# Multiplying half of the value chunks in 32 bits, unsplit, with a column of ones

## The chip, the cores and the metric

The kernel runs on one core of one Trainium2 chip. TensorE (PE) multiplies and writes its results to PSUM, VectorE (DVE) and ScalarE (ACT) compute on SBUF and PSUM, GpSimd (POOL) on SBUF alone, and SyncE (SP) issues nearly all DMAs. The metric is the device time of one execution in microseconds.

## What is computed

The reference is an attention through 49 agents in two steps, followed by a mixture of experts. There are 4 batches of 10048 tokens with 128 channels.

```python
a2k = sm(agents, k)          # softmax over the 10048 keys, with the scale 1/sqrt(128)
agent_v = a2k @ v            # 49 x 128 for each batch
q2a = sm(q, agents)          # softmax over the 49 agents
x = (q2a @ agent_v).reshape(B * N, D)
...
# each token goes to one group of four and one expert of four in it
h = np.maximum(xg[mask_e] @ w1[g, e], 0.0)
ye = h @ w2[g, e]
out[tok_idx] = combined[:, None] * ye
```

The change concerns `a2k @ v`: the sum over all keys of the weight of a key for each agent, times the value of that key, and the sum of the weights by which it is divided.

## The kernel before

The 10048 tokens of a batch are 79 tiles of 128 (the last one has 64), in 8 chunks of 10 tiles (the last of 9). The batches are taken in the order 1, 2, 3, 0. Precision comes from splitting: a 32-bit operand is written as a 16-bit part and a 16-bit remainder, and a product is the sum of three 16-bit products (high x high, high x low, low x high).

*The opening.* For the first batch everything is computed alone: `front` runs keys and values in an order written out by hand (`ORDER`). There the values are not split: `key_exp` loads a chunk of values to `vf`, of 129 columns, and sets the last column to one; `key_values` multiplies each tile in 32 bits, weights `S` (128 keys x 49 agents) stationary and `vf` moving, so that the product has 49 rows of 128 channels and the sum of the weights.

*The stream.* Then the expert layer of batches 1, 2 and 3 runs as a stream of units (`first`, `evicted`, `second`): two products of 512 columns into a bank `ph`, an eviction in two parts (`hh` by ScalarE, `hl` by VectorE), and three products of 512 columns into `po`. A batch has 20 tiles of 8 units. There are three `ph` banks, so TensorE runs at most three units ahead of the evictions. After each unit `advance` steps generators ("lanes") that prepare later batches: the keys and values of the next batch (`k1`, `k2`, `k3`), the queries (`q0` to `q3`), and what follows them. `QUEUE` says from which to which part of the stream a lane runs, `TOTALS` how much weighted work it has in all, `RATE` how much VectorE and ScalarE work one unit may take; `behind` compares the done share with the share of the window. After that a planner draws up every engine's queue anew, from the order of emission and its own estimate of when each operand is there; operations of one engine can change places in it.

*A k lane* is `agents`: `key_load` and `key_scores` for all chunks, `key_max`, and then for all chunks four stages run skewed by one chunk each: `value_load` (DMA to `vf`, two buffers) and `value_less` (subtract the maximum), `value_exp`, `value_split` and `value_products`. `value_split` writes `vh` and `sh` (ScalarE), `vl` in two pieces a chunk (VectorE), `sl` in two pieces (GpSimd), and adds the weights of chunks 1 to 7 onto those of chunk 0 in two pieces a chunk (GpSimd). `value_products` makes three products a tile, values stationary (128 x 128) and weights moving (49 columns), into the bank `acc`, 128 channels x 49 agents. At the end `agents` sums the weights over the 10 tiles of chunk 0 and over partitions by a product with ones, and divides. Only these three lanes are touched by the change; the opening isn't.

*The last batch* is sorted by expert and computed with gathered rows and scattered results, after the three streamed ones.

A helper records nearly all operations, so most rows carry its line, L137, and are told apart by their tiles.

Of the kernel before, what the change touches and what calls it, by code (L numbers as in the profile page):

```python
# [10 lines left out]
F32 = mybir.dt.float32  # L11
# [3 lines left out]
ALU = mybir.AluOpType  # L15
# [52 lines left out]
ORDER = "kkkkkmkvkvqkqmvvqvvvv"  # L68
RATE = np.array([900.0, 1100.0])
POOLED = "01001001"  # L70
KA = 2
QUEUE = (("a0", 0.0, 9.0), ("a1", 0.0, 9.0), ("a2", 0.0, 9.0), ("a3", 0.0, 9.0),
         ("q0", 0.0, 0.50), ("k1", 0.0, 0.60), ("q1", 0.40, 1.35), ("k2", 0.60, 1.15), ("q2", 1.30, 2.35), ("k3", 1.15, 1.70), ("q3", 1.55, 2.25), ("p3", 1.80, 2.72))
TOTALS = {"q0": 22.9e3, "k1": 55.1e3, "q1": 26.2e3, "k2": 55.1e3, "q2": 26.2e3, "k3": 55.1e3, "q3": 26.2e3, "p3": 79.0}
WL = (0.5, 1.0, 0.7)
AHEAD = 4
AHEAD_TURNS = 2
# [64 lines left out]
def build(ctx, tc, qT, kT, v, agT, wr, w1, w2, cpk, out, cols):  # L142
# [28 lines left out]
    def bank(any_=True):  # L171

        if wide[0] and any_:
            turns[0] += 1
            k = turns[0] % 8
            if k in (0, 3, 6):
                return ps1.tile([P, TS], F32, name="ph")
            if k in (1, 4):
                return ps2.tile([P, TQ, C], F32, name="po").rearrange("p a c -> p (a c)")
        return psa.tile([P, 512], F32, name="at", tag="at")  # L180
# [20 lines left out]
    vec.memset(ones16, 1.0)  # L201
    ones = const.tile([P, P], F32, name="ones")
    vec.memset(ones, 1.0)
    shift = const.tile([P, 1], F32, name="shift")
    vec.memset(shift, float(np.log(ES)))
    keep = const.tile([P, NE, ST], F16, name="keep")
# [222 lines left out]
    def value_load(b, ci):  # L429

        t0, t1 = chunks[ci]
        vf = stg.tile([P, CT, C + 1], F32, name="vf", tag="vf", bufs=2)
        nf = min(t1, NT - 1) - t0
        sync.dma_start(out=vf[:, 0:nf, 0:C], in_=v[b, t0 * P:(t0 + nf) * P].rearrange("(t p) c -> p t c", p=P))
        if t1 == NT:
            sync.dma_start(out=vf[0:LAST, nf, 0:C], in_=v[b, (NT - 1) * P:N])
        state[b]["v", ci] = vf
        yield

# [18 lines left out]
    def value_split(b, ci):  # L458

        st = state[b]  # L460
        vf = st.pop(("v", ci))
        sh, sl = [mo.tile([P, CT, NA], F16, name=name) for name in ("sh", "sl")]
        vh, vl = [wk.tile([P, CT * P], F16, name=name, tag="x" + name[1]).rearrange("p (t c) -> p t c", c=C) for name in ("vh", "vl")]
# [25 lines left out]
    def value_products(b, ci):  # L489

        st = state[b]
        sh, sl, vh, vl = st.pop(("v", ci))
        if ci == 0:
            st["acc"] = bank(False)
        acc = st["acc"]
        t0, t1 = chunks[ci]
        for t in range(t0, t1):
            m = min(P, N - t * P)
            i = t - t0
            for x, y in (vh, sh), (vh, sl), (vl, sh):  # L500
                pe.matmul(acc[:, 0:NA], x[0:m, i], y[0:m, i], start=(t == 0 and x is vh and y is sh), stop=False)
            if i % 5 == 4 or t == NT - 1:
                yield
        yield

    def agents(b):
# [5 lines left out]
        yield from skewed(n, lambda ci: both(value_load(b, ci), value_less(b, ci)), lambda ci: value_exp(b, ci), lambda ci: value_split(b, ci), lambda ci: value_products(b, ci))  # L512
        yield
        acc = st["acc"]
        sums = sm.tile([P, NA], F32, name="mx")
        vec.tensor_reduce(out=sums, in_=st["S"][:, 0:CT].rearrange("p t a -> p a t"), axis=AX.X, op=ALU.add)
        yield HOP
        pe.matmul(acc[:, NA:2 * NA], ones, sums, start=False, stop=True)
        yield HOP
        za = sm.tile([P, NA], F32, name="za2")  # L520
        vec.tensor_scalar(out=za, in0=acc[:, NA:2 * NA], scalar1=1e-9 * ES, scalar2=None, op0=ALU.add)
        vec.reciprocal(out=za, in_=za)
        avT = sm.tile([P, NA], F32, name="avT")
        vec.scalar_tensor_tensor(out=avT, in0=acc[:, 0:NA], scalar=1.0 / VS, in1=za, op0=ALU.mult, op1=ALU.mult)
        yield
        yield from agents_scaled(b, avT)

# [1080 lines left out]
```

## Time and profile before

| what | value |
|---|---|
| median of 3 runs (lowest to highest) | 939.1 us (936.59 to 939.77) |
| the profiled execution | 946.72 us |
| its span from first to last instruction | 945.0 us |
| TensorE busy, weight loads busy | 860.7 us (91%), 511.9 us |
| VectorE busy | 750.0 us (79%) |
| ScalarE busy | 623.1 us (66%) |
| GpSimd busy | 468.5 us (50%) |
| mean granted TensorE clock | 0.975 |

Durations of instructions come from the profiled execution, and so does every sum of them. A matmul's record contains its drain, so the records of short matmuls overlap, and the busy time of TensorE hides short waits; the distance from start to start tells what one costs in a run. The granted clock is a share of full speed: 1.0 is 2.4 GHz, 0.5 is 1.2 GHz.

### The profile page before, as it was taken

The numbers are of one execution on the slowest core, as the hardware profiler recorded it, in microseconds if no ns is written. First come the engines' busy times: TensorE is split into PE (matmuls) and PEld (weight loads), VectorE is DVE, ScalarE is ACT, GpSimd is POOL, SyncE is SP. The second block draws the span as 40 slices with busy tenths as digits, with TensorE's granted clock in tenths as the row PEclk, the third lists the DMA queues.
The fourth block names the chain that finished last, engine by engine and source line by source line (L and its number), as shares of the span: only waits on it lengthen the run. The fifth ranks groups of instructions, "written<-read, shape, count | busy, mean of one in ns | idle before, by whom it ended". The sixth has DMA issues, their size and how long they took to land.

```text
span 945.0 us, 22657 instructions
## 1 busy us (share of the span) xinstructions
PE 860.7 (91%) x8616; PEld 511.9 (54%) x8617; DVE 750.0 (79%) x1621; ACT 623.1 (66%) x1084; POOL 468.5 (50%) x618
## 2 busy tenths in 40 slices
PE   3878998999999889989799989999999999999994
PEld 2763554544555445544445555544444467777774
DVE  5647799898689898859988998989997666666662
ACT  4546787776878777768679867766566554555551
POOL 3164656653747343476547423656555414444444
PEclk9977999999999999989999999999999999999998
DMA  9637743746435554553534233333576435455542
GB/s 316 182 127 241 240 128 91 227 146 201 141 110 188 166 170 134 182 159 115 168 122 158 92 125 96 99 124 108 173 255 221 148 133 175 152 184 186 173 153 66
DMA packets 96495, 150.63 MB, mean 159 GB/s; under 512 B 8984, under 2 KB 61843, under 8 KB 96377
## 3 DMA queue, kind: packets, MB, share of 16 engines
q1 hardware_dynamic: 91225, 138.80, 46.0%
q0 software_dynamic: 5152, 10.30, 3.3%
q8 instruction: 69, 1.13, 0.5%
q14 instruction: 49, 0.40, 0.1%
HBM read 108.04 MB, written 39.69 MB: 156 GB/s over the span
## 4 chain that ended last, share of the span: by engine, by line
PE 54%; DVE 23%; issue 7%; POOL 7%; ACT 5%; DMA 3%; SPq 0%; POOLq 0%; ACTq 0%; DVEq 0%
PE po L137 28%; PE ph L137 16%; PE at L137 10%; DVE hl L137 8%; POOL xl L273 3%; DVE vl L137 3%; ACT hh L137 2%; POOL out L1286 2%; DVE oh L137 2%; DVE S L137 1%; DVE oo L137 1%; DVE mq L137 1%; ACT vh L137 1%; DVE ef L137 1%; POOL xs L273 1%
## 5 line engine op out<-in xcount | busy, mean ns | idle before, releaser
L137 DVE SCALAR_TENSOR_TENSOR hl<-ph,hh 128x512 f16<-128x512 f32 (+1 forms) x562 | 376.0, 676 | 127.6 <-ACT hh L137 111.3
L137 ACT ACTIVATE hh<-ph 128x512 f16<-128x512 f32 (+1 forms) x562 | 328.4, 592 | 194.2 <-PE ph L137 102.1
L137 PEld LDWEIGHTS <-wbuf 128*128 128x128 f16 (+2 forms) x2852 | 246.6, 98 | 297.8 <-issue 59.6
L137 PE MATMUL ph<-et,wbuf 98*128 98x512 f16 (+2 forms) x1048 | 319.1, 379 | 23.1 <-DVE hl L137 21.3
L137 PE MATMUL po<-hh,wbuf 128*128 128x512 f16 (+1 forms) x960 | 288.0, 379 | 2.7 <-DVE oo L137 2.1
L273 POOL TENSOR_TENSOR xl<-xf,xh 128x256 f16<-128x256 f32 x280 | 188.0, 706 | 154.5 <-ACT xh L137 144.3
L137 PE MATMUL po<-hl,wbuf 128*128 128x512 f16 (+1 forms) x480 | 181.7, 378 | 0.0
L1286 POOL DMA_INDIRECT out<-oo,er x82 | 80.4, 981 | 113.3 <-ACT hh L137 55.1
L137 PE MATMUL po<-wbuf,hh 128*128 128x128 f16 x1312 | 117.1, 219 | 0.5 <-issue 0.5
L137 PE MATMUL po<-wbuf,hl 128*128 128x128 f16 x656 | 113.0, 219 | 0.3 <-issue 0.2
L1013 POOL DMA_INDIRECT sorted_rows<-rows,slot x79 | 80.0, 1012 | 62.6 <-ACT hh L137 36.5
L137 PEld LDWEIGHTS <-hh 128*128 128x128 f16 x1312 | 99.2, 98 | 9.4 <-issue 9.3
L137 ACT ACTIVATE xh<-xf 128x1280 f16<-128x1280 f32 (+2 forms) x59 | 73.7, 1251 | 20.6 <-PE at L137 8.0
L137 PEld LDWEIGHTS <-xh 128*128 128x128 f16 (+1 forms) x1164 | 58.8, 99 | 23.3 <-issue 5.3
L719 POOL TENSOR_TENSOR rows<-ef,rows 128x245 f16<-128x245 f32 (+1 forms) x62 | 39.9, 666 | 60.7 <-ACT rows L137 60.7
L137 PEld LDWEIGHTS <-hl 128*128 128x128 f16 x656 | 64.2, 98 | 0.9 <-issue 0.9
L480 POOL TENSOR_TENSOR sl<-S,sh 128x245 f16<-128x245 f32 (+2 forms) x51 | 36.2, 733 | 51.5 <-ACT sh L137 40.1
L137 PE MATMUL at<-agh,xl 128*128 128x49 f16 x523 | 52.7, 186 | 5.6 <-POOL xl L273 5.4
L137 DVE SCALAR_TENSOR_TENSOR hl<-at,hh 128x512 f16<-128x512 f32 x82 | 55.8, 681 | 0.0
L137 PE MATMUL at<-agh,xh 128*128 128x49 f16 x523 | 52.7, 186 | 2.0 <-DVE base L137 1.4
L137 PEld LDWEIGHTS <-xl 128*128 128x128 f16 x582 | 48.9, 98 | 7.6 <-POOL xl L273 7.2
L137 ACT ACTIVATE et<-at 98x512 f16<-98x512 f16 (+2 forms) x80 | 47.2, 593 | 7.8 <-PE at L137 7.7
(277 smaller groups left out, 1188.5 us busy)
## 6 DMA issues: line engine op xcount, KB each, us to landing
wbuf<-wdr SPq DMA_DIRECT2D x22, 832.0 KB
vf<-v SPq DMA_DIRECT2D x28, 640.0 KB
xf<-qT SPq DMA_DIRECT2D x28, 640.0 KB
cols<-oo SPq DMA_DIRECT2D x60, 256.0 KB
xf<-kT SPq DMA_DIRECT2D x23, 640.0 KB
oo<-cwt SPq DMA_DIRECT2D x57, 256.0 KB
erow<-rows SPq DMA_DIRECT2D x12, 490.0 KB
er<-sorted_rows SPq DMA_DIRECT2D x19, 256.0 KB
```

The costliest lines, as they stand in the source:

```text
L137: return f(*a, **k)
L273: pool.tensor_sub(out=xl[:, a:z], in0=xf[:, a:z], in1=xh[:, a:z])
L480: pool.tensor_sub(out=sl[0:m, y][:, z], in0=x[:, z], in1=sh[0:m, y][:, z])
L719: pool.tensor_sub(out=x0[:, a:z, NA:2 * NA], in0=ef[:, a:z], in1=x0[:, a:z, 0:NA])
L1013: ins = pool.indirect_dma_start(out=sorted_rows[:, :], out_offset=bass.IndirectOffsetOnAxis(ap=at, axis=0), in_=x, in_offset=None, bounds_ ...
L1286: ins = pool.indirect_dma_start(out=out, out_offset=bass.IndirectOffsetOnAxis(ap=to, axis=0), in_=y, in_offset=None, bounds_check=N - 1, o ...
```

## The change

Of the eight chunks of values of each later batch, those with a "1" in `WHOLE` (1, 3, 4 and 6, ten tiles each) are no longer split. `value_load` sets the 129th column of their `vf` to one, `value_split` does nothing for them, and `value_products` multiplies `S` (stationary, 49 columns) with `vf` (moving, 129 columns) in 32 bits, one product a tile, into other columns and the first 49 rows of the same PSUM bank. The other four chunks go as before. GpSimd no longer adds the weights of the four chunks onto chunk 0; the column of ones gives their sum. At the end of a batch the 49 x 129 result is copied to SBUF, transposed and scaled by a product with `identv`, its sums are spread over the partitions by a product of ones with a diagonal matrix, and both are added to what the split chunks gave. `TOTALS` of the three k lanes is 46.8e3 instead of 55.1e3. A manual dependency without a semaphore keeps the first 32-bit product behind the one that opens the bank.

```diff
--- before.py
+++ after.py
@@ -68,10 +68,11 @@
 ORDER = "kkkkkmkvkvqkqmvvqvvvv"
 RATE = np.array([900.0, 1100.0])
 POOLED = "01001001"
+WHOLE = "01011010"
 KA = 2
 QUEUE = (("a0", 0.0, 9.0), ("a1", 0.0, 9.0), ("a2", 0.0, 9.0), ("a3", 0.0, 9.0),
          ("q0", 0.0, 0.50), ("k1", 0.0, 0.60), ("q1", 0.40, 1.35), ("k2", 0.60, 1.15), ("q2", 1.30, 2.35), ("k3", 1.15, 1.70), ("q3", 1.55, 2.25), ("p3", 1.80, 2.72))
-TOTALS = {"q0": 22.9e3, "k1": 55.1e3, "q1": 26.2e3, "k2": 55.1e3, "q2": 26.2e3, "k3": 55.1e3, "q3": 26.2e3, "p3": 79.0}
+TOTALS = {"q0": 22.9e3, "k1": 46.8e3, "q1": 26.2e3, "k2": 46.8e3, "q2": 26.2e3, "k3": 46.8e3, "q3": 26.2e3, "p3": 79.0}
 WL = (0.5, 1.0, 0.7)
 AHEAD = 4
 AHEAD_TURNS = 2
@@ -201,6 +202,8 @@
     vec.memset(ones16, 1.0)
     ones = const.tile([P, P], F32, name="ones")
     vec.memset(ones, 1.0)
+    identv = const.tile([NA, NA], F32, name="identv")
+    vec.tensor_scalar(out=identv, in0=identf[0:NA, 0:NA], scalar1=VS, scalar2=None, op0=ALU.mult)
     shift = const.tile([P, 1], F32, name="shift")
     vec.memset(shift, float(np.log(ES)))
     keep = const.tile([P, NE, ST], F16, name="keep")
@@ -434,6 +437,8 @@
         sync.dma_start(out=vf[:, 0:nf, 0:C], in_=v[b, t0 * P:(t0 + nf) * P].rearrange("(t p) c -> p t c", p=P))
         if t1 == NT:
             sync.dma_start(out=vf[0:LAST, nf, 0:C], in_=v[b, (NT - 1) * P:N])
+        if WHOLE[ci] == "1":
+            vec.memset(vf[:, :, C:C + 1], 1.0)
         state[b]["v", ci] = vf
         yield
 
@@ -458,6 +463,9 @@
     def value_split(b, ci):
 
         st = state[b]
+        if WHOLE[ci] == "1":
+            yield
+            return
         vf = st.pop(("v", ci))
         sh, sl = [mo.tile([P, CT, NA], F16, name=name) for name in ("sh", "sl")]
         vh, vl = [wk.tile([P, CT * P], F16, name=name, tag="x" + name[1]).rearrange("p (t c) -> p t c", c=C) for name in ("vh", "vl")]
@@ -489,16 +497,28 @@
     def value_products(b, ci):
 
         st = state[b]
+        t0, t1 = chunks[ci]
+        if WHOLE[ci] == "1":
+            vf = st.pop(("v", ci))
+            for t in range(t0, t1):
+                m = min(P, N - t * P)
+                ins = pe.matmul(st["acc"][0:NA, P:P + C + 1], st["S"][0:m, t], vf[0:m, t - t0], start=False, stop=False)
+                if t == t0:
+                    tc.add_manual_dep(ins.ins, st["opened"].ins.name, mybir.DependencyInfo(mybir.DependencyClass.NoSync, mybir.DependencyReason.DATA),
+                                      reason="the bank is opened by the first product")
+                if (t - t0) % 3 == 2 or t == t1 - 1:
+                    yield
+            return
         sh, sl, vh, vl = st.pop(("v", ci))
         if ci == 0:
             st["acc"] = bank(False)
         acc = st["acc"]
-        t0, t1 = chunks[ci]
         for t in range(t0, t1):
             m = min(P, N - t * P)
             i = t - t0
             for x, y in (vh, sh), (vh, sl), (vl, sh):
-                pe.matmul(acc[:, 0:NA], x[0:m, i], y[0:m, i], start=(t == 0 and x is vh and y is sh), stop=False)
+                ins = pe.matmul(acc[:, 0:NA], x[0:m, i], y[0:m, i], start=("opened" not in st), stop=(t == NT - 1 and x is vl))
+                st.setdefault("opened", ins)
             if i % 5 == 4 or t == NT - 1:
                 yield
         yield
@@ -512,16 +532,25 @@
         yield from skewed(n, lambda ci: both(value_load(b, ci), value_less(b, ci)), lambda ci: value_exp(b, ci), lambda ci: value_split(b, ci), lambda ci: value_products(b, ci))
         yield
         acc = st["acc"]
+        af = sm.tile([NA, C + 1], F32, name="af", bufs=1)
+        vec.tensor_copy(out=af, in_=acc[0:NA, P:P + C + 1])
+        dg = sm.tile([NA, NA], F32, name="dg")
+        vec.tensor_scalar(out=dg, in0=identf[0:NA, 0:NA], scalar1=af[:, C:C + 1], scalar2=None, op0=ALU.mult)
         sums = sm.tile([P, NA], F32, name="mx")
         vec.tensor_reduce(out=sums, in_=st["S"][:, 0:CT].rearrange("p t a -> p a t"), axis=AX.X, op=ALU.add)
         yield HOP
-        pe.matmul(acc[:, NA:2 * NA], ones, sums, start=False, stop=True)
+        ps = bank()
+        pe.matmul(ps[:, 0:NA], af[:, 0:C], identv, start=True, stop=False)
+        pe.matmul(ps[:, NA:2 * NA], ones, sums, start=False, stop=False)
+        pe.matmul(ps[:, NA:2 * NA], ones[0:NA, :], dg, start=False, stop=True)
         yield HOP
         za = sm.tile([P, NA], F32, name="za2")
-        vec.tensor_scalar(out=za, in0=acc[:, NA:2 * NA], scalar1=1e-9 * ES, scalar2=None, op0=ALU.add)
+        vec.tensor_scalar(out=za, in0=ps[:, NA:2 * NA], scalar1=1e-9 * ES, scalar2=None, op0=ALU.add)
         vec.reciprocal(out=za, in_=za)
         avT = sm.tile([P, NA], F32, name="avT")
-        vec.scalar_tensor_tensor(out=avT, in0=acc[:, 0:NA], scalar=1.0 / VS, in1=za, op0=ALU.mult, op1=ALU.mult)
+        vec.tensor_copy(out=avT, in_=acc[:, 0:NA])
+        vec.tensor_add(out=avT, in0=ps[:, 0:NA], in1=avT)
+        vec.scalar_tensor_tensor(out=avT, in0=avT, scalar=1.0 / VS, in1=za, op0=ALU.mult, op1=ALU.mult)
         yield
         yield from agents_scaled(b, avT)
```

## Rows read from the trace of the kernel before

**Rows 1.** Stretches: their length, busy us and instructions by engine, granted clock, DMA.

```profile
128.00:214.00 86.00, 77.41 (x819) 42.81 (x817) 79.89 (x151) 67.12 (x116) 53.03 (x73) 0.98 0.50 152
214.00:282.00 68.00, 65.99 (x641) 35.70 (x637) 54.26 (x124) 50.54 (x84) 35.31 (x56) 1.00 0.46 148
282.00:354.00 72.00, 64.83 (x607) 35.13 (x604) 67.46 (x132) 55.59 (x95) 37.50 (x51) 0.98 0.56 173
354.00:430.00 76.00, 69.88 (x651) 37.29 (x651) 56.16 (x118) 51.62 (x84) 35.69 (x58) 0.93 0.50 152
430.00:500.00 70.00, 63.46 (x605) 33.14 (x605) 65.89 (x115) 53.29 (x90) 43.04 (x56) 0.98 0.48 142
500.00:685.00 185.00, 176.51 (x1519) 93.82 (x1518) 171.20 (x469) 132.57 (x241) 93.77 (x122) 1.00 0.37 120
```

**Rows 2.** Who ended waits of TensorE, 128 to 214 us: total, times, longest.

```profile
PE ph L137 <- DVE hl L137: 4.2, 6, 2.3
```

**Rows 3.** The same, 282 to 355 us.

```profile
PE ph L137 <- DVE hl L137: 4.2, 5, 2.6
PE at L137 <- DVE vl L137: 2.5, 2, 2.0
```

**Rows 4.** The same, 430 to 500 us.

```profile
PE ph L137 <- DVE hl L137: 5.4, 5, 1.8
PE at L137 <- DVE vl L137: 0.9, 2, 0.4
```

**Rows 5.** Timeline of TensorE (start us, us, instruction): fifteen f16 value products, the next.

```profile
138.76 0.19 PE L137 MATMUL at<-sh,vh 128*128 128x49 f16 x1
...
139.14 0.59 PE L137 MATMUL ph<-et,wbuf 98*128 98x512 f16 x2
```

**Rows 6.** Timeline of ScalarE; in brackets the idle time before and its releaser.

```profile
310.01 1.27 ACT L137 ACTIVATE vh<-vf 128x1280 f16<-128x1280 f32 x1 [2.45 <-DMA vf<-v]
```

**Rows 7.** Timeline of VectorE, the same time.

```profile
311.31 0.82 DVE L137 SCALAR_TENSOR_TENSOR vl<-vf,vh 128x640 f16<-128x640 f32 x1 [1.85 <-ACT vh L137]
```

**Rows 8.** Timeline of TensorE, the same time.

```profile
312.65 0.59 PE L137 MATMUL ph<-et,wbuf 98*128 98x512 f16 x2 [2.60 <-DVE hl L137]
```

**Rows 9.** Timeline of TensorE in the opening, a run of f32 products.

```profile
44.99 5.18 PE L137 MATMUL at<-vf,S 128*49 128x129 f32 x45
```

**Rows 10.** Tile vf: count, duration ns min/median/max, first and last start us, forms.

```profile
L137 PE MATMUL at<-vf,S x158: 270/273/453, 31.7 to 55.5; 128*49 128x129 f32 x156, 64*49 64x129 f32 x2
...
L137 DVE MEMSET vf<- x8: 67/67/67, 1.7 to 47.0; 128x10 f32 x8
```

**Rows 11.** Tile sh, the same columns.

```profile
L137 PE MATMUL at<-sh,vh x237: 183/185/248, 138.8 to 499.3; 128*128 128x49 f16 x117, 64*128 64x49 f16 x2
```

**Rows 12.** Groups by shape, TensorE: busy us, mean ns | idle before.

```profile
L137 PE MATMUL at<-mx,ones 128*128 128x49 f32 x6 | 1.0, 240 | 0.0
```

**Rows 13.** The same, VectorE, 128 to 500 us.

```profile
L137 DVE SCALAR_TENSOR_TENSOR vl<-vf,vh 128x640 f16<-128x640 f32 x45 | 45.4, 1015 | 3.7 <-ACT vh L137 3.6
```

**Rows 14.** The same, ScalarE, 128 to 500 us.

```profile
L137 ACT ACTIVATE vh<-vf 128x1280 f16<-128x1280 f32 x21 | 26.6, 1268 | 6.3 <-PE at L137 2.8 <-DMA vf<-v 2.4 <-DVE ef L137 0.9
...
L137 ACT ACTIVATE sh<-S 128x490 f16<-128x490 f32 x21 | 12.9, 616 | 0.9 <-PE at L137 0.9
```

**Rows 15.** The same, GpSimd, 128 to 500 us.

```profile
L485 POOL TENSOR_TENSOR S<-S 128x245 f32<-128x245 f32 x39 | 33.5, 882 | 13.7 <-ACT S L137 13.7
L480 POOL TENSOR_TENSOR sl<-S,sh 128x245 f16<-128x245 f32 x45 | 32.8, 749 | 51.5 <-ACT sh L137 40.1 <-PE ph L137 11.5
```

**Rows 16.** Timeline of VectorE around 332 us.

```profile
331.82 1.34 DVE L137 SCALAR_TENSOR_TENSOR vl<-vf,vh 128x640 f16<-128x640 f32 x1 [0.69 <-ACT vh L137]
```

**Rows 17.** Timeline of GpSimd, the same time.

```profile
330.55 3.78 POOL L273 TENSOR_TENSOR xl<-xf,xh 128x256 f16<-128x256 f32 x5 [1.64 <-PE at L137]
```

**Rows 18.** Waits of the DMA queue on SyncE, 120 to 500 us.

```profile
SPq L434 <- DVE vl L137: 40.1, 15, 7.9
```

**Rows 19.** Waits of VectorE in the opening, 0 to 60 us.

```profile
DVE vf L137 <- PE at L137: 3.3, 3, 2.5
```

## The prediction, made before the change was run

> **What bounds the kernel now.** I first read the busy time by stretch [rows 1], because the share over the whole span mixes an opening, three streamed batches and a sorted batch. Three stretches hold the value phases that the change touches: 128 to 214, 282 to 354 and 430 to 500 us, 228 us together. The reader is to see two things. TensorE is busy 77.41 + 64.83 + 63.46 = 205.7 us of them, so it stands still for 22.3 us, and its granted clock is 0.98 in each, which is 2% of 228 = 4.6 us more. VectorE is busy 79.89 + 67.46 + 65.89 = 213.2 us, 94%. In the neighbours 214 to 282 and 500 to 685 us TensorE stands still only for 2.0 of 68 us (3.0%) and 8.5 of 185 us (4.6%), at a clock of 1.00. So the value phases are the worst served part of the stream, and VectorE is the fullest engine there.
>
> Then I read who ended TensorE's waits in these stretches [rows 2 to 4]. Waits of `ph` for the eviction `hl` are 4.2 + 4.2 + 5.4 = 13.8 us in 16 pieces, waits of `at` for `vl` 2.5 + 0.9 = 3.4 us in 4. Both are VectorE's: 17.2 us in 20 waits. The record of a 49-column matmul lasts 0.18 us where the next one starts 0.025 us later [rows 5], so every wait hides about 0.16 us behind the drain: 20 x 0.16 = 3.2 us more, 20.4 us in all. The whole loss of the value phases is 22.3 + 4.6 + 3.2 = 30.1 us.
>
> How one such wait arises is seen at 310 us: ScalarE stands 2.45 us in front of `vh` until the values have landed [rows 6], VectorE takes the 0.82 us `vl` behind it before the evictions in its queue [rows 7], and TensorE stands 2.60 us for `hl` [rows 8]. Counted in order, two long `vl` to a chunk, this is chunk 3, one of the four that the change leaves unsplit.
>
> **The change: TensorE pays.** 40 tiles a batch, 120 in three, lose three f16 products of 49 columns and gain one f32 product of 129. In the opening the kernel already makes this f32 product: 45 records in 5.18 us; less the last one's 0.27 us this is 44 starts in 4.91 us, 111.6 ns each [rows 9, 10]. But one product is two records: 158 matmuls stand for the 79 tiles of one batch [rows 10], whereas the f16 product has 237 for 3 x 79 [rows 11]. So a tile costs 2 x 111.6 = 223 ns. Its three f16 products cost 139.14 - 138.76 = 0.38 us for 15, 25.3 ns each, 76 ns a tile [rows 5]. The difference is 147 ns x 120 = 17.6 us. At the end of a batch two more f32 products (the transposed sum, the diagonal) are four records; six comparable ones keep TensorE 1.0 us, 0.17 us each [rows 12]: 4 x 0.17 x 3 = 2.0 us. TensorE gets **19.6 us** more, all in the value stretches.
>
> The Trainium skill would make this another sum: "Perfetto Trace Analysis", section Engine Utilization, gives TensorE half its rate for FP32_LOW_HIGH. By that alone a tile would cost 2 x 129 columns, an estimate of 108 ns, and TensorE would get only some 6 us more. The two records a tile say that the rate is halved twice here; I go by them.
>
> **What the other engines lose.** *VectorE:* two `vl` in each of 12 chunks. 45 of them take 45.4 us, 1.01 us each [rows 13]: 24 x 1.01 = 24.2 us go. New are 12 memsets of ten columns, 0.067 us each [rows 10], 0.8 us, and four small steps at a batch's end (copy of the sum, diagonal, copy, add). Their forms aren't in the trace; between that memset and the 0.82 us of a `vl` [rows 7] I take 0.2 us, as they have at most 129 columns: 2.4 us, bounds 0.8 and 9.8. Net 21 us less, which takes VectorE from 94% to 84% of the stretches. *ScalarE:* `vh` 1.268 and `sh` 0.616 us [rows 14], 12 x 1.884 = 22.6 us less. *GpSimd:* two `sl` of 0.749 and two sums of 0.882 us a chunk [rows 15], 24 x 1.631 = 39 us less; the column of ones does those sums now, inside the f32 product. None of these three is time by itself; each counts as far as TensorE waited for it.
>
> **What comes back.** Lower bound: half the `vl` go, so half of the waits for VectorE, 10.2 us, with half of the lost clock, 2.3: 12.5 us. Upper bound: all that waits for VectorE and all the clock, 20.4 + 4.6 = 25.0 us. Between them stands the nearest neighbour: 214 to 282 us runs with VectorE at 54.26 of 68 us, 80%, close to the 84% to come. If TensorE's idle share falls to that stretch's 3.0%, 6.8 us of the 22.3 stay; 15.5 come back, with the clock's 4.6 and some 1.9 of what drains hide 22.0 us; by 500 to 685 us (4.6%) it is 18.3. I take **23.5 us**, nearer to the top, because the largest wait of the second stretch falls wholly on an unsplit chunk, and because TensorE's own added work fills part of the waits for other things that remain (5.1 us: 22.3 less 17.2). A wait that is filled so costs nothing, and its price is back where VectorE isn't behind.
>
> **The sum.** 19.6 - 23.5 = -3.9 us. Against the profiled execution (946.72 us, span 945.0, 1.7 us around it) that is 942.8 us. This execution is 7.6 us above the median of the runs, 939.1; the difference is carried over to it: **935.2 us**.
>
> **Costed at nothing.** The manual dependency orders two TensorE products that are in order already. `identv` is one small VectorE step among the constants. TOTALS falls from 55.1e3 to 46.8e3 with the lane's work, in the same windows, so the values still end where they did; if a lane fell late, the cover is the time until its batch is needed; for the third that is from its last value product, 499.3 us [rows 11], to the end of the streamed batches near 685 us [rows 1], 186 us. The f32 weight loads (0.124 us) lie beside the 512-column products and each other, as in the opening, whose 111.6 ns contain them.
>
> **A wait that moves.** An unsplit chunk keeps its `vf` buffer until its products, not until `vl`; there are two buffers. The load of the chunk two later (chunks 3, 5 and 6) stands on SP behind the products. SP already stands 40.1 us in 15 waits for `vl` there [rows 18]; behind it are queued the loads of `xf` and of the factors `oo`, for which VectorE waits, and the stores. The memset stands on VectorE for the same buffer; behind it are the evictions `hl`, for which TensorE waits. In the opening, where the same memset waits for products, it stood 3.3 us in three waits, up to 2.5 [rows 19]. Twelve of 1.1 us would be 13 us of VectorE's time; the bounds are 0 and 13 and I take 0, because in these stretches VectorE lags and TensorE has gone ahead. The price of the other end is rival 2.
>
> **Rivals.** *1. TensorE becomes the bound (slower).* The place is the value stretches, the price 19.6 us of columns, and it decides as soon as less than 19.6 us of waits return. For it: the four split chunks keep their `vl`, so their bursts stay, and the half that is sure returns 12.5 us. Against it: the neighbours at 3.0 to 4.6% idle. With 12.5 to 19 us back it is +7.1 to +0.6, 946 to 940 us.
>
> *2. The buffer comes late.* Chunk 5 is split and its load waits for chunk 3's products. If ScalarE stands in front of its `vh` as in [rows 6], TensorE loses 2.60 us [rows 8] a batch, 7.8 us in three: 943 us. For it: that wait exists already. Against it: the loads before chunks 3 and 6 feed no split any more.
>
> *3. More returns.* With ScalarE 22.6 and GpSimd 39 us freer, the waits outside VectorE shrink as well, the 5.1 us and some in the next stretches: 27 to 34 us back, 932 to 925 us. For it: with GpSimd at work (a run of `xl` from 330.55 for 3.78 us [rows 17]) a `vl` took 1.34 us [rows 16] instead of 0.82, so less GpSimd work shortens the `vl` that stay. The Trainium skill, "GPSIMD Engine Reference", section Specifications, says that the SBUF interfaces are shared with VectorE and collide with its instructions that have two SBUF inputs; `vl` is one. By that rule rival 3 gets more weight; the two rows agree with it. Against it: only 24 `vl` stay, at most 0.19 us each above 0.82, 4.6 us.
>
> *4. The product goes out as one record*, at 111.6 ns a tile: 13.4 us less, 922 us. The skill's half rate, above, is this case; 158 records for 79 tiles speak against it.
>
> **How the numbers follow.** Forecast (21 to 26 us back, 938 to 933 us) 0.40; rival 1 0.27; rival 2 0.13; rival 3 0.18; rival 4 0.02. About 0.3%, 2.8 us, is what a measurement can tell from no change: faster is below 936.3, slower above 941.9. Faster: 0.30 of the forecast, rivals 3 and 4, 0.50. Same: 0.10 of the forecast, 0.10 of rival 1, 0.03 of rival 2, 0.23. Slower: 0.17 + 0.10 = 0.27. The range is 926 to 946: it leaves out the far parts of rival 3, rival 4 and, above, the cases in which rivals 1 and 2 meet. As both signs hold much, the forecast's own range is 933 to 938.
>
> **What would show it.** Right: 80 records of f32 products a batch beside 39 x 3 f16 ones; a pitch of 112 ns in runs of six; VectorE near 84% in the value stretches, TensorE's idle share there near 3% and the clock at 1.00. Wrong: `ph` still waiting some 10 us for `hl` (rival 1); waits of ScalarE for `vf` or of VectorE's memset for TensorE (rival 2); a pitch far from 112 ns. What is weakest is the 23.5: the order of every engine's queue is planned anew, and a new order brings waits of its own.

## The result, and the profile after

The changed kernel is slower: 943.45 us median (941.38 to 944.47) against 938.7 us (936.59 to 940.29) beside it, a ratio of 1.0051 (95%: 1.0035 to 1.0066). That is 4.7 us in the direction that the prediction gave 0.27. The profiled execution took 943.06 us; that this lies beside the 942.8 us of the sum says nothing, because the execution of before that was profiled was itself 8 us longer than its median.

First the page of the changed kernel: span, then busy time, share of the span and instructions of each engine.

```profile
span 941.3 us, 22362 instructions
...
PE 876.7 (93%) x8508; PEld 523.5 (56%) x8509; DVE 726.0 (77%) x1622; ACT 606.9 (64%) x1060; POOL 420.7 (45%) x570
```

TensorE is busy 16.0 us longer than in the table before, VectorE 24.0, ScalarE 16.2 and GpSimd 47.8 us shorter. So the work moved about as it was meant to. The stretches, with the columns of [rows 1], cut at the value phases of the changed kernel (lines 1, 3 and 5):

```profile
132.00:222.00 90.00, 83.99 (x766) 46.07 (x765) 70.91 (x151) 60.91 (x103) 33.65 (x51) 0.98 0.48 149
222.00:286.00 64.00, 61.35 (x599) 33.30 (x597) 51.36 (x115) 46.84 (x80) 35.15 (x56) 1.00 0.42 134
286.00:357.00 71.00, 67.80 (x562) 37.98 (x561) 60.96 (x139) 48.26 (x83) 26.30 (x40) 1.00 0.63 192
357.00:426.00 69.00, 64.78 (x618) 34.72 (x615) 55.66 (x107) 47.99 (x81) 33.34 (x53) 0.98 0.50 149
426.00:498.00 72.00, 69.42 (x596) 37.92 (x596) 56.05 (x114) 49.11 (x83) 30.62 (x47) 1.00 0.46 137
```

VectorE fell from 94% to 79, 86 and 78% of the value phases, TensorE's idle time in them from 22.3 to 6.0 + 3.2 + 2.6 = 11.8 us. Here are the waits of TensorE for the evictions, which were [rows 2 to 4] before, for the three value phases in order:

```profile
PE ph L138 <- DVE hl L138: 2.1, 4, 1.1
```
```profile
PE ph L138 <- DVE hl L138: 2.6, 3, 1.9
```
```profile
PE ph L138 <- DVE hl L138: 1.7, 1, 1.7
```

13.8 us in 16 waits became 6.4 us in 8, and the waits of `at` for `vl` are gone. By these two views the kernel should be faster. What they can't show is what TensorE spends its busy time on, and that is where the time is. The 32-bit products by shape, TensorE and its weight loads, 120 to 500 us (busy us, mean ns | idle before, and its releasers):

```profile
L138 PE MATMUL at<-vf,S 128*49 128x129 f32 x240 | 35.4, 280 | 0.3 <-DMA vf<-v 0.3
...
L138 PEld LDWEIGHTS at<-vf,S 128*49 128x49 f32 x240 | 24.1, 123 | 12.4 <-issue 11.3 <-DMA vf<-v 0.4
```

240 records for 120 tiles, as forecast. But the weight loads stood 12.4 us, 11.3 of them for nothing that the trace names. One run in the timeline of TensorE (start us, us, instruction):

```profile
299.79 0.38 PE L138 MATMUL po<-hl,wbuf 128*128 128x512 f16 x1
300.10 0.86 PE L138 MATMUL at<-vf,S 128*49 128x129 f32 x6
300.90 0.39 PE L138 MATMUL ph<-et,wbuf 98*128 98x512 f16 x1
```

The six records follow each other every 110 ns. The first of them starts 0.31 us behind a product of 512 columns, where the next such product would start 0.215 us behind it, and the next kind of product starts 0.204 us behind the last one instead of 0.110. Changing to a stationary side of 49 columns costs 93 ns here and changing back 95 ns, also between products of 49 moving columns (114 ns instead of 25). There are 88 such changes in the stream, and in 84 of them nothing else stands in the gap: 7.7 us.

**A ledger.** The distances from start to start of TensorE's records, less what a product of that shape takes in an unbroken run (25 ns for 49 columns in 16 bits, the columns at 2.4 GHz and 2 ns for longer ones, 110 ns for a 32-bit record of 129 columns), split the stream from the first eviction `hl` to the 481st, where the streamed batches end, into four terms. *Switch* is the excess under 120 ns where a run of unsplit products begins or ends; *clock* is what products took longer in stretches at 1.2 GHz; *waits* are the rest. One profiled execution each, in us:

| kernel | stream | work | switch | clock | waits |
|---|---|---|---|---|---|
| before (second execution) | 679.8 | 610.6 | 0 | 6.2 | 62.6 |
| before (the one in front) | 681.9 | 610.6 | 0 | 10.2 | 60.8 |
| after | 683.7 | 628.5 | 7.7 | 3.4 | 44.1 |
| after (second execution) | 685.7 | 628.5 | 7.8 | 3.0 | 45.9 |
| e2_price | 692.2 | 628.5 | 0 | 5.0 | 58.4 |
| e3_relief | 672.3 | 608.7 | 7.6 | 7.3 | 48.3 |
| e4_two | 680.2 | 619.8 | 4.3 | 4.6 | 51.1 |
| e5_long | 687.2 | 628.5 | 2.2 | 10.2 | 45.7 |
| e6_single | 694.3 | 628.5 | 10.5 | 8.9 | 46.1 |
| e7_bufs | 686.3 | 628.5 | 7.8 | 6.7 | 43.3 |
| e8_wide | 670.9 | 608.7 | 0.3 | 6.0 | 55.9 |
| e9_long_free | 685.0 | 628.5 | 2.2 | 9.3 | 45.1 |
| e10_free | 682.0 | 628.5 | 7.6 | 1.4 | 44.1 |
| e11_wide_free | 661.1 | 608.7 | 0.2 | 4.5 | 47.4 |
| e12_no_vl | 667.6 | 610.6 | 0 | 4.7 | 51.9 |
| e13_before_bufs | 677.6 | 610.6 | 0 | 5.8 | 60.8 |
| e14_wide_late | 675.6 | 608.7 | 0.4 | 8.7 | 57.9 |
| e16_narrow_free | 664.9 | 608.7 | 7.9 | 4.4 | 43.7 |
| e17_wide_again | 658.8 | 608.7 | 0.3 | 1.6 | 47.8 |
| e18_f32_128 | 679.3 | 628.5 | 0 | 3.2 | 47.3 |

From before to after: +17.9 of work, +7.7 of switching, -2.8 of clock, -18.5 of waits, together +4.3 (+3.9 by the stream's ends; some records are missing). The clock term differs by 4 us between two executions of one kernel, so a single row is good to some 4 us; verdicts go by the medians. How much of a lower clock ends up in the time is read from the runs: over all of them, each held against the mean of its own kernel, 0.01 of the mean granted clock goes with 1.8 us of time. That is an estimate; single kernels scatter widely around it.

### The profile page after: what moved, and what is told of

Same layout as the page of the kernel before. It is cut to its first block, busy times and chain, and to the rows that moved or that the text cites. A ratio compares the mean times of both kernels' runs of the same rounds, so it can differ in the third digit from the quotient of the medians.

```text
span 941.3 us, 22362 instructions
## 1 busy us (share of the span) xinstructions
PE 876.7 (93%) x8508; PEld 523.5 (56%) x8509; DVE 726.0 (77%) x1622; ACT 606.9 (64%) x1060; POOL 420.7 (45%) x570
## 4 chain that ended last, share of the span: by engine, by line
PE 60%; DVE 22%; DMA 6%; ACT 5%; issue 4%; POOL 2%; SPq 1%; POOLq 0%; ACTq 0%; DVEq 0%
PE po L138 30%; PE ph L138 17%; PE at L138 13%; DVE hl L138 8%; DMA vf<-v 2%; ACT hh L138 2%; DVE oo L138 1%; DVE oh L138 1%; DMA out<-oo,er 1%; DVE rx L138 1%; DVE rd L138 1%; DVE S L138 1%; POOL xs L276 1%; DVE ef L138 1%; DVE mq L138 1%
## 5 line engine op out<-in xcount | busy, mean ns | idle before, releaser
L276 POOL TENSOR_TENSOR xl<-xf,xh 128x256 f16<-128x256 f32 x280 | 182.3, 686 | 231.6 <-ACT xh L138 230.8
L748 POOL TENSOR_TENSOR rows<-ef,rows 128x245 f16<-128x245 f32 (+1 forms) x62 | 39.9, 666 | 67.9 <-ACT rows L138 63.1
L138 PEld LDWEIGHTS <-xh 128*128 128x128 f16 (+1 forms) x1164 | 56.9, 98 | 21.5 <-issue 4.5
L138 PE MATMUL at<-vf,S 128*49 128x129 f32 x398 | 55.7, 284 | 1.7 <-ACT S L138 1.5
L138 PE MATMUL at<-agh,xh 128*128 128x49 f16 (+1 forms) x523 | 51.1, 185 | 3.0 <-DVE most L138 2.4
L138 PE MATMUL at<-agh,xl 128*128 128x49 f16 (+1 forms) x523 | 51.3, 184 | 1.6 <-POOL xl L276 1.5
L138 PEld LDWEIGHTS at<-vf,S 128*49 128x49 f32 x398 | 42.9, 127 | 14.6 <-issue 11.5
```

The costliest lines, as they stand in the source:

```text
L138: return f(*a, **k)
L276: pool.tensor_sub(out=xl[:, a:z], in0=xf[:, a:z], in1=xh[:, a:z])
L748: pool.tensor_sub(out=x0[:, a:z, NA:2 * NA], in0=ef[:, a:z], in1=x0[:, a:z, 0:NA])
```

## The experiments

Kernels were timed on several chips, on which the kernel before took 938 to 945 us; each ratio is to the kernel before on the same chip.

**Is the noise as small as thought?** e1_before_again is the kernel before, unchanged.

> The kernel before, unchanged, profiled once more. Theory A: the profiled execution on which the sum was made (946.72 us) held some 8 us of waits that an ordinary execution doesn't hold, so a new trace has a span near 937 us, with TensorE idle some 15 us instead of 22.3 in the three value stretches. Theory B: profiled executions of this kernel are always near 945 us, and the trace was typical; then the span is again near 945 us with about 22 us idle there, and the sum failed in its own terms. The ratio of times is 1.000 by both.

937.02 us, ratio 0.9987 (0.9971 to 1.0004): no change, as it must be. The span of its trace is 937.0 us, as theory A has it, but TensorE stands still for 22.0 us in the three value stretches of [rows 1], as in the trace in front (22.3) and not for 15. So the 8 us lay elsewhere (2.1 us of them in the stream, by the ledger, the rest outside it), and the prediction read its value phases from a typical trace.

**What does TensorE's price cost alone?** e2_price leaves the kernel before as it is and adds products into columns that nobody reads.

```diff
+            if EXTRA[ci] == "1":
+                for _ in range(2 if i == 0 else 1):
+                    more = nc.tensor.matmul(acc[:, P:P + NE * ST], ident, keep.rearrange("p e t -> p (e t)"), start=False, stop=False)
```

> The kernel before with TensorE's added work alone: 11 more f16 products of 320 columns (0.136 us each, 18.0 us in all three batches) in each of the chunks 1, 3, 4 and 6, into columns nobody reads; all splitting stays. If TensorE is the bound of the value stretches, all 18 us are paid: 957 us. If VectorE is, its lag absorbs most of it: 941 to 944 us. If the parts add up, this run less the kernel before, plus the run with the relief alone, gives the 4.7 us of the change.

952.43 us, 1.0148 (1.0125 to 1.0170): 14 of 18 us are paid. Added columns don't vanish in the waits of the value phases: TensorE is a bound there, though VectorE is at 94%.

**What comes back if TensorE pays nothing?** e3_relief multiplies only the upper 16 bits of `S` and `vf`, so that a tile is one record, and leaves out the lower ones; e8_wide has 128 stationary columns besides, of which 49 are used.

```diff
-                ins = pe.matmul(st["acc"][0:NA, P:P + C + 1], st["S"][0:m, t], vf[0:m, t - t0], start=False, stop=False)
+                ins = nc.tensor.matmul(st["acc"][0:NA, P:P + C + 1], st["S"].bitcast(BF16)[0:m, t, 1::2], vf.bitcast(BF16)[0:m, t - t0, 1::2], start=False, stop=False)
```

> The changed kernel with the products of the unsplit chunks made from the upper 16 bits of weights and values, one product of 129 columns a tile in 16 bits (about 56 ns, where the kernel before needs 76 and the changed one 223); the lower 16 bits are left out, so the result is coarser, and no token changes its expert. This is the relief of VectorE, ScalarE and GpSimd without TensorE's price (2.4 us less instead of 17.6 us more). Theory A (about 15 us come back): 939 - 15 - 2 = 922 us. Theory B (23.5 us come back, as forecast): 939 - 23.5 - 2 = 913 us. If little comes back without the price, about 930 us: then the price had been filling waits.

931.48 us, 0.9928 (0.9902 to 0.9955): only 6.8 us back. With the 14.1 us of e2_price that makes +7.3 us, where the change measures +4.7: price and relief don't simply add up.

> The kernel with the relief alone (e3: products from the upper 16 bits), but with a stationary operand of 128 columns instead of 49; the further 79 columns are those of the next tiles and their results are read by nobody. If the switch comes from the width of the stationary, the 93 ns in front of a run and the 95 ns behind it are gone, TensorE gets 7.6 us less, and with half of it paid the time is 3 to 6 us below e3: 925 to 929 us. If it comes from the operands' type or their stride, it stays, and the time is that of e3, 931 us. Lower 16 bits are left out here too.

935.09 us, 0.9950 (0.9926 to 0.9974). The switching is gone (7.6 to 0.3 us) and the waits grew by as much, so the 3 to 6 us that were expected below e3_relief didn't come. Waits for `hl` grew most (10.1 to 13.8 us in 120 to 500 us). One kind of wait is new for TensorE against the kernel before, and longer for ScalarE, in e3_relief (4.6 and 9.3 us) as in e8_wide. Its lines in e8_wide, 120 to 500 us (total, times, longest):

```profile
PE at L507 <- DMA vf<-v: 5.9, 2, 3.2
```
```profile
ACT vh L139 <- DMA vf<-v: 9.9, 5, 4.1
```

Both stand for values whose load waits for one of the two `vf` buffers, rival 2's mechanism. e14_wide_late and e17_wide_again take it apart: both write the ones two stages later, when the load has landed; e17_wide_again (and its first run, e11_wide_free) has a third buffer.

```diff
-        vf = stg.tile([P, CT, C + 1], F32, name="vf", tag="vf", bufs=2)
+        vf = stg.tile([P, CT, C + 1], F32, name="vf", tag="vf", bufs=3)
...
-        if WHOLE[ci] == "1":
-            vec.memset(vf[:, :, C:C + 1], 1.0)
...
         if WHOLE[ci] == "1":
+            vec.memset(st["v", ci][:, :, C:C + 1], 1.0)
             yield
             return
```

> e8_wide (16-bit halves, 128 stationary columns, so that TensorE pays nothing for the change: 742.6 us of work in the stream against 744.5 before, 0.3 us of switching) with three vf buffers and the ones written late. The lower 16 bits of weights and values are left out in the four chunks. It measures what comes back by itself. The prediction's 23.5 us would be a ratio of 0.975. In e8_wide, at 0.995, TensorE waited 2.9 and 3.3 us for loads of vf that stood for a buffer; with those gone I expect 0.988 to 0.992, so about 10 us. If it stays at 0.995 the buffers were no cause either, and only 5 us come back.

927.46 us, 0.9802 (0.9769 to 0.9834).

> e11_wide_free once more, as the base for e16_narrow_free and e14_wide_late on the same chip. Its first result was 0.9802 (0.9769 to 0.9834); expected 0.977 to 0.984. With the changed kernel beside it, the difference of the two is TensorE's whole price, 19.6 us of work and 7.7 us of switching: 27 us if it is paid in full, 12 to 15 us if half of it lies in waits.

921.22 us, 0.9771 (0.9739 to 0.9803).

> e8_wide (two vf buffers) with the ones written late, so that between it and e17_wide_again only the third buffer stands, and between it and e8_wide only the place of the memset. In e8_wide TensorE waited 5.9 us and ScalarE 9.9 us for loads of vf, and TensorE 0.7 us behind the memset. So I expect the buffer to be most of the 14 us between e8_wide and e11_wide_free: 0.990 to 0.995 here. If the memset is most of it, 0.980 to 0.985.

936.67 us, 0.9929 (0.9906 to 0.9953). So it is the buffer, not the memset. (The expert weights `w2f`, six loads, share the buffers and get the third one too.) With it out of the way 19 to 22 us come back, and TensorE no longer waits for `vf`. The 742.6 and 744.5 us of work named above are not the ledger's 608.7 and 610.6, but their difference is the same. All that is left of waits over 1 us in e17_wide_again, 120 to 500 us:

```profile
PE ph L139 <- DVE hl L139: 14.9, 18, 2.0
PE at L139 <- DVE ef L139: 3.3, 3, 1.2
PE at L139 <- DVE most L139: 2.9, 1, 2.9
```

> The kernel before without vl in the same four chunks; vh stands in its place, so that the low part of those values is left out and TensorE's, ScalarE's and GpSimd's work stays. TOTALS of the three lanes falls to 49.25e3 with the work. VectorE alone loses 24 us. The prediction put nearly all of the return to VectorE: then 17 to 20 us come back, a ratio of 0.979 to 0.982. If the waits come from the order of the queues and from chains across engines more than from VectorE's fullness, the ratio is 0.992 or above.

e12_no_vl skips `vl` and puts `vh` in its place in the products, which so count twice; the rest is the kernel before. 933.15 us, 0.9887 (0.9851 to 0.9923): 10.7 us for 24 us of VectorE, less than the 17 to 20 expected and more than the other theory's 8. That is half of what all the split work returns with three buffers, but more than the 5 to 7 us that it returns with two. And e12_no_vl also gives the `vf` buffer back earlier, behind `vh`: SyncE's 40.1 us of waits for `vl` became 20.9 for `vl` and 12.1 for `vh`. So what VectorE's fullness costs by itself stays open.

**Does the switching cost time, and what makes it?** e16_narrow_free is e17_wide_again with 49 stationary columns.

> e11_wide_free with 49 stationary columns instead of 128 (as in e3_relief): the same columns for TensorE, the same work elsewhere, three vf buffers, ones written late; only the switching between 128 and 49 stationary columns comes in, 7.6 us by the records of e3_relief. If TensorE is the bound once the buffers are no cause, it pays it nearly in full: 6 to 8 us over e17_wide_again, a ratio some 0.007 higher. If the waits beside it take it up, it is within 2 us of it.

930.42 us, 0.9876 (0.9845 to 0.9908), 9.2 us above e17_wide_again on the same chip for 7.6 us of switching by the records. The mean granted clock of its runs is 0.974 against 0.981, some 1 us by the estimate above; what is left is the switching, paid in full. e18_f32_128 gives the true 32-bit product 128 stationary columns (with three buffers and the late ones, as e10_free):

```diff
-                ins = pe.matmul(st["acc"][0:NA, P:P + C + 1], st["S"][0:m, t], vf[0:m, t - t0], start=False, stop=False)
+                ins = pe.matmul(st["acc"][:, P:P + C + 1], st["S"].rearrange("p t a -> p (t a)")[0:m, t * NA:t * NA + P], vf[0:m, t - t0], start=False, stop=False)
```

> e10_free with 128 stationary columns for the 32-bit products too: the 49 weights of the tile and the first 79 of the tiles behind it; the 49 rows that are used are the same. If it is the number of stationary columns that makes the switch cost, it vanishes as in e8_wide (7.6 to 0.3 us), and the ratio falls from 1.005 to 0.996 to 0.999. If 32-bit weights pay it whatever their number, it stays at 1.005, and if the longer weight loads (209 ns for 128 columns against 136 for 49 in the kernel before) don't fit beside the 110 ns of a record, it is slower: 240 records a kernel at 20 ns more are 5 us, 1.010.

942.45 us, 1.0018 (1.0002 to 1.0035): by the ratios 6 us under e10_free, from which it differs by the width alone, 3 under the changed kernel, and 2, within the intervals, under e7_bufs below. Its timeline, at a place like the one shown of the changed kernel, and its two rows by shape, 120 to 500 us:

```profile
157.31 0.38 PE L138 MATMUL po<-hl,wbuf 128*128 128x512 f16 x1
157.53 0.83 PE L138 MATMUL at<-vf,S 128*128 128x129 f32 x6
158.20 0.60 PE L138 MATMUL ph<-et,wbuf 98*128 98x512 f16 x2
```
```profile
L138 PEld LDWEIGHTS at<-vf,S 128*128 128x128 f32 x240 | 32.0, 191 | 3.6
...
L138 PE MATMUL at<-vf,S 128*128 128x129 f32 x240 | 34.9, 280 | 0.0
```

The run starts 0.22 us behind the long product and lasts 0.67 instead of 0.80 us. Each weight load takes 191 instead of 123 ns, and yet the records still come every 110 ns and the loads' idle time falls from 12.4 to 3.6 us. So the switch hangs on the 49 columns, not on the 32 bits.

The Trainium skill, "TensorE: Matmul & The Clock Gate", section "Weight-path perf modes — Fast Weight Load (FWL) and DoubleRow", says that weights load fast when there are 128 of them and the type is not FP32. The durations of the loads agree: 98 ns for 128 columns in 16 bits, 126 ns for the 98 columns of `rows`, 191 ns for 128 columns in 32 bits. The switch doesn't follow them: e18_f32_128 has the slowest of these loads and no switch.

Nor does every other width switch. In the changed kernel transposes with 98 stationary columns and products with 64 stand among products with 128 (start us, us, instruction):

```profile
349.66 0.38 PE L138 MATMUL po<-hl,wbuf 128*128 128x512 f16 x1
349.87 0.39 PE L138 MATMUL at<-ident,rows 128*98 128x128 f16 x4
350.09 0.60 PE L138 MATMUL ph<-et,wbuf 98*128 98x512 f16 x2
```
```profile
272.65 0.18 PE L138 MATMUL at<-agh,xl 128*128 128x49 f16 x1
272.77 0.21 PE L138 MATMUL at<-agh,xh 128*64 128x49 f16 x1
...
272.85 0.19 PE L138 MATMUL at<-agh,xl 128*64 128x49 f16 x1
272.98 0.39 PE L138 MATMUL ph<-et,wbuf 98*128 98x512 f16 x1
```

The transposes start 0.215 us behind the long product and the next product 0.055 us behind the last of them: nothing is lost. The products with 64 columns start 114 ns after the one before, instead of 25, and the next starts 123 ns after the last, instead of 31. The products over the 64 keys of a batch's last tile pay as much (116 and 112 ns instead of 25), with all 128 columns stationary. The kernel before has all these rows too. What decides which shapes pay was not tried.

**Can the switching be avoided by longer runs?** In e5_long all ten tiles of a chunk go in one run, in e6_single each tile may stand alone.

```diff
-                if (t - t0) % 3 == 2 or t == t1 - 1:
+                if t == t1 - 1:
```

> The changed kernel with the ten f32 products of a chunk in one run instead of in threes. Theory S (switching): going from 128-column stationaries to the 49-column ones and back costs TensorE 93 + 95 ns, 7.7 us in some 44 runs of the changed kernel, which the sum left out; in 12 runs it is 2.3 us, so TensorE gets 5.4 us less and 2 to 5 us come back: 938.5 to 941.5 us. Theory R (only the relief was overrated, switching is idle time anyway): no change, or slower because a run of 2.2 us delays the expert units: 943 to 947 us.

948.23 us, 1.0070 (1.0045 to 1.0095). The switching fell to 2.2 us in 24 changes, and nothing was gained. TensorE's waits, 120 to 500 us, name one reason: VectorE stood with the memset for the buffer, with evictions behind it.

```profile
PE ph L138 <- DVE vf L138: 3.2, 1, 3.2
...
PE at L138 <- DVE vf L138: 1.9, 1, 1.9
```

> The changed kernel with each tile's f32 product alone among expert units: up to 120 runs instead of 44. Theory S: 76 more switches of 0.188 us, 14.3 us of TensorE, of which 6 to 14 us are paid: 949 to 957 us. Theory R: 943 to 945 us.

956.18 us, 1.0157 (1.0129 to 1.0185): 124 changes instead of 88, 10.5 us of switching. Of the 10 us over the changed kernel the ledger puts 2.8 to switching and more to the clock. The sign is as expected, the size isn't explained by the switching alone.

> The changed kernel with the ten 32-bit products of a chunk in one run, three vf buffers, and the ones written two stages later, beside value_split, when the load has landed. In e5_long the long run took 5.5 us of switching away (7.7 to 2.2 us in 24 changes), but VectorE's memset of the ones stood for the buffer with the evictions behind it: TensorE lost 2.1 us behind it in the first value stretch and 3.4 us in the second. If the buffer is what ate the gain, those waits vanish and the time is some 5.5 us under e10_free, about the time of the kernel before (ratio 0.998 to 1.000). If switching costs no time because TensorE would only wait longer, it stays within 2 us of e10_free.

950.72 us, 1.0052 (1.0030 to 1.0075), against e10_free with short runs:

> The changed kernel with three vf buffers and the ones written late, the 32-bit products in runs of three tiles as in the changed kernel. Beside e9_long_free it isolates the length of the runs, beside e7_bufs the place of the memset. The buffer waits of TensorE in the changed kernel are 0.7 us behind the memset and 0.4 us behind a load, so both theories expect 0 to 2 us less than the changed kernel: ratio 1.002 to 1.005.

952.53 us, 1.0080 (1.0049 to 1.0111). 1.8 us less for 5.4 us of switching, and the intervals overlap. TensorE's waits behind the memset are gone, though VectorE itself still stood 6.7 us in three waits for the products that held the buffer. The mean granted clock in all runs is 0.974 in both kernels with long runs (7 and 12 runs), against 0.978, 0.980 and 0.980 in e10_free, e7_bufs and the changed kernel (6, 12 and 12). By the estimate from the runs, half a per cent of the clock is some 1 us, a part of the 3.6 us that are missing. Whether the long runs lower the clock was not tried, and why they gain so little stays open; e9_long_free isn't told apart from e10_free.

**Do the buffers hold the changed kernel back?**

> The changed kernel with three buffers for the values instead of two, so that the load two chunks later no longer waits for the unsplit chunk's products. If the buffer kept until the products costs time (rival 2 of the prediction), some 3 to 8 us come back: 935 to 940 us. By theories S and R the buffer isn't what binds: 942 to 945 us.

945.52 us, 1.0036 (1.0015 to 1.0058), and e10_free no better: no. The third buffer is worth 14 to 15 us where TensorE is quick (e8_wide to e11_wide_free, e14_wide_late to e17_wide_again) and nothing that can be told where TensorE pays 27 us more. There TensorE waits only 0.3 us for values; ScalarE waits 5.7 us for them, and still 5.4 us with the third buffer.

> The kernel before with three vf buffers instead of two, nothing else. In the run of the kernel before, SyncE stood 40.1 us in 15 waits for vl with the next load of vf, and ScalarE stood once 2.6 us for a load before vh. If the buffer holds the kernel before as it held e8_wide, 3 to 6 us come back (ratio 0.994 to 0.997), and the return measured in e17_wide_again is partly the buffer's own gain. If the loads are early enough, 1.000 within 0.002.

937.76 us, 0.9967 (0.9948 to 0.9986): 3 us less by the ratio, though the interval overlaps the 0.9971 to 1.0004 of the unchanged kernel in e1_before_again, so the gain is barely clear of noise. The 2.4 us in which ScalarE stood for `vf` [rows 6] are gone. SyncE's waits for `vl` stayed (39.9 us in 15), and TensorE's waits in the ledger, 60.8 us, are those of the trace in front.

**Is half as much better?** e4_two leaves only chunks 3 and 6 unsplit (`WHOLE = "00010010"`, `TOTALS` 50.95e3).

> The changed kernel with two unsplit chunks (3 and 6) instead of four, TOTALS 50.95e3. If price and relief both go with the number of chunks, half the change: 941 us. If the first unsplit chunks take away the largest waits and the further ones only add columns, 935 to 938 us, below the kernel before. If the loss comes from the end of a batch (the extra products and copies, the same with two chunks), 943 us.

941.25 us, 1.0042 (1.0020 to 1.0064): no better than four chunks within the intervals.

**And the changed kernel again,** on the chip of e14, e16 and e17:

> The changed kernel once more, on the chip of the three runs beside it, so that they can be held against it directly. Its first result was a ratio of 1.0051 (1.0035 to 1.0066); every theory expects 1.003 to 1.008.

947.0 us, 1.0049 (1.0029 to 1.0069), the first result once more.

## Why the prediction was wrong, point by point

- **The step that failed** is in "Costed at nothing": the f32 weight loads "lie beside the 512-column products and each other, as in the opening". Beside each other they do; at each change between 128 and 49 stationary columns TensorE stands. That is 7.7 us of TensorE, put at nothing. With it the sum would have been -3.9 + 7.7 = +3.8 us, against +4.7 measured; part of that closeness is luck, because the work was 1.7 us less than forecast and the return 2 to 4 us less. How much of the 7.7 us the changed kernel pays is bracketed and not shown: e16_narrow_free pays all of it, e18_f32_128 got 2 to 6 us back by removing it, and the long runs, which remove 5.5, got 2 us or nothing. The trace in front had the row: I took the pitch from a run of 45 and didn't look at its ends. The opening, timeline of TensorE in the kernel before:

```profile
43.05 0.60 PE L137 MATMUL at<-vf,S 128*49 128x129 f32 x4
43.58 0.42 PE L137 MATMUL ph<-ident,rows 128*98 128x128 f16 x4
43.94 0.42 PE L137 MATMUL at<-vf,S 128*49 128x129 f32 x2
```

  Four records at 110 ns would free TensorE after 0.44 us; the next product starts after 0.53.
- **TensorE's price** of 19.6 us was right: two records a tile, 110 ns (forecast 111.6), 17.9 us of work by the ledger with the batch ends. The half rate that the other sum went by holds for a record (110 ns, against some 58 ns for the 16-bit record of 129 columns in e3_relief) and not for a product, which is two.
- **What comes back** was forecast as 23.5 us. By the ledger waits and clock fell by 18.5 + 2.8 = 21.3 us, or 19.9 in the second executions of both, inside the bounds and 2 to 4 us short. But its reason was half wrong: it isn't a number of VectorE's, which the change can draw down. Freed of `vl` alone the kernel before gains 10.7 us for 24; freed of all the split work with TensorE unburdened, 5 to 7 us with two buffers and 19 to 22 with three. That it is 21 us in the changed kernel is in part because TensorE's own added time fills waits, as the prediction said of 5.1 us: by the ledger waits and clock fall by 5.4 us in e2_price, with the price alone, and by 13.2 us in e3_relief, with the relief alone.
- **Rival 1** is what happened: TensorE became the bound. Its point of decision, 19.6 us of returned waits, was too low by the switching, 27.3; the return of 20 to 21 us lies between the two. Even the upper bound of the return, 25.0, lies below the true point, so with the switching in the sum rival 1 would have been the forecast.
- **Rival 2** (the buffer) costs TensorE little in the changed kernel: TensorE waits 0.3 us for a load, and 0.5 us, once, for an eviction behind the memset. One of its signs did come: ScalarE waits 5.7 us in five pieces for `vf`, 2.4 us in one before; but e7_bufs with its third buffer is no faster. SyncE's waits moved as told: 40.1 us for `vl` [rows 18] became 17.7 for `vl` and 21.8 for products. It is real where TensorE is quicker, in e8_wide. In the kernel before I had a row of it [rows 6] and priced it only as a thing that the change might add; there a third buffer is worth 3 us by the medians, barely clear of noise.
- **Rival 3** was right in one detail: the `vl` that stay take 886 ns instead of 1015 [rows 13], with less of GpSimd beside them, as the section Specifications of "GPSIMD Engine Reference" in the Trainium skill would have it. That is 21 x 0.13 = 2.7 us of VectorE and was not enough. **Rival 4** is out: 240 records.
- **The other engines:** VectorE 23 us less on the page than in the second execution of before (forecast 21), GpSimd 48 (39), ScalarE 16 (22.6). Of ScalarE's records the forecast was right: those of `vh` fell from 26.6 to 11.4 us and of `sh` from 12.9 to 5.6, 22.5 us; the page counts the time of overlapping records once.
- **The signs named beforehand:** VectorE near 84% came (79 to 86), the pitch of 112 ns came, the clock of 1.00 in two of three stretches; TensorE's idle share is 3.6 to 6.7% and not 3. "`ph` still waiting some 10 us" was to show rival 1; it waits 6.4. The sign that told it, a pitch at the ends of the runs, was not on the list.

## What to carry to other kernels

Price an operation on TensorE by the starts before and behind its run, not only by the pitch inside: here a stationary side of 49 columns among 128 cost at both ends, and widening it with columns that nobody reads took that away at no cost that the records show. What waits return is no property of the engine that is relieved; measure the price alone and the relief alone, in two runs, and don't expect them to add up exactly (+7.3 us here, for +4.7). And where a loaded tile's buffer count is two, look for the engine that stands for its load: with TensorE unburdened a third buffer was worth 14 to 15 us.

## What the runs showed of the hardware

- A change between products with 128 and with 49 stationary columns costs TensorE 93 ns on the way in and 95 ns on the way out, in 16 bits (e3_relief, e16_narrow_free) as in 32; within a run of either kind nothing.
- In the changed kernel products with 64 stationary columns, and products over 64 keys with 128 columns, pay 87 to 92 ns at either end, too; transposes with 98 columns pay nothing.
- Weight loads of 128 columns of 32 bits, 191 ns each, run beside records at a pitch of 110 ns, no slower than those of 49 columns at 123 ns.
- A 32-bit product of 129 columns is two records of 110 ns, whether 49 or 128 columns are stationary.
- Two executions of the kernel before differ by 4.0 us in what the granted clock cost them in the stream (6.2 and 10.2 us), by the time that it stood at 1.2 GHz, with the same work and nearly the same waits.
